# A table of selected rows in 112 rows, a searched order of work, and products of the identity in TensorE's gaps: block-sorted attention and a Fourier-mixing MLP

## The chip, the core and the metric

The kernel runs on one core of one Trainium2 chip. The engines have short names here: PE is TensorE's matmul side and PEld its weight loads, DVE is VectorE, ACT is ScalarE, POOL is GpSimd, SP is SyncE, which issues DMAs only. The metric is the device time of one execution in microseconds, as the median over runs: lower is better. The profile is of one execution, and its times count from the first instruction. PEclk in a profile is the share of TensorE's clock that was granted.

## What is computed

The reference has two halves. The first is attention in blocks: of 4 batches and 8 heads, each with 768 tokens of 64 features, the tokens are cut into 8 blocks of 96. A small 8 by 8 matrix per head is normalised five times by rows and columns and mixes the blocks of k and v; then each block of q attends to its mixed block. The second half takes the 512 features of all heads, adds the real part of a two-dimensional Fourier transform (over tokens and features), normalises each token, and runs an MLP of width 2048.

```python
for _ in range(5):
    P = np.exp(P - P.max(-1)); P = P / P.sum(-1); P = P / P.sum(-2)
k_sorted = einsum('bhij,bhjcd->bhicd', P, k_b)      # v likewise
attn = softmax(scale * q_b @ k_sorted.T)            # per block of 96
x = (attn @ v_sorted) as (4, 768, 512)
u = x + real(fft(fft(x, axis=1), axis=2))
un = (u - mean(u)) / sqrt(var(u) + 1e-6)
out = u + maximum(un @ w_ch1, 0) @ w_ch2
```

(The lines are shortened; the reference keeps the dimensions and adds 1e-9 to the sums.)

## The kernel before, in words

The kernel does not issue its work in the order of its source. Each piece (a few instructions on one engine) is given to a planner with `step` or `chain`: a name, the batch, the engines that could do it with a duration in nanoseconds for each, what it reads and what it writes. When all steps are known, `run` (L344) plays the program with its own clock: it keeps a time at which each engine is free, one for each DMA queue, and the buffers of each ring, and takes again and again the step that can start first, or of several within 40 ns (`NEAR`) the one of least priority number. `emit` (L279) then issues the step's instructions for good, so the order on each engine's queue is this order. The engines wait for each other through semaphores; the planner's times only decide the order and, where a step may run on several engines, the engine.

The priority of a step is its batch times 1e5 less the length of the work that hangs on it, plus 1000 times an entry of the table `LEAD` (L203), which holds for each name of a step four numbers, one for each batch. The entries are the result of a search.

The stages of a batch: k, q and v are loaded (`load_kq` on POOL's queue, `load_v` on SP's, L502), v is cast to half precision (`v_cast`, on ACT or DVE) and summed on POOL, the mixing matrix is spread out (`kron`), products with it give the mixed v and k (`psV`, `psK`, copies `vo`, `kz`), scores are computed twice (`psS` for the maxima, `psT` with the maximum taken off), ACT takes the exponentials (`exp`, tile `sm`), one is subtracted (`minus`, tile `eT`), POOL or DVE copies eight columns (`twice`, L850), and products with v give the attention (`psN`, L856). The Fourier transform over tokens folds the rows (`fold`, `fold2`) and multiplies with constant tables (L903), the one over features follows (L947 to L957). Then a row selection brings x into the order of the transform (`residual`, L984 and L987, with the constant table `rsel`), POOL adds (L1007, L1008), DVE takes mean and variance, `un` normalises (DVE, ACT or POOL, L1050 and L1053), the result is turned on PE (L1076) or by a DMA, and the MLP runs in two groups of 384 tokens (L1104 and L1125, with `relu` on ACT in between). MLP steps have the weakest priority: they fill what TensorE has free.

The table `rsel` is a constant in DRAM of 107 rows (96 + 11), each with 4 selections of 97 columns in half precision. It shares the tile `room` with small tables of the start, and is loaded by `load_const` (L1172) on SP's queue, not before 27 us of the planner's clock. Its price in the plan is `6 * elements // 1000 + 50` ns of transfer. Its rows 96 to 106 pick the mean rows; the products read 105 to 107 rows.

PSUM is eight banks of 512 columns. The ring `bank` hands them out singly and `pair` in twos; `open()` lists the free ones by the time at which they came free.

Early in the kernel, `warm` issues products of a tile of ones into bank 7, in three places before the planner's run starts.

Of the kernel before, what the change touches and what calls it, by code (L numbers as in the profile page):

```python
# [10 lines left out]
F16 = mybir.dt.float16  # L11
# [9 lines left out]
BLK = 96  # L21
G = 6
# [23 lines left out]
def _consts():  # L46

    p = np.arange(128)
    mask16 = (p[:, None] % 16 == np.arange(16)[None, :]).astype(np.float32)

    dd = np.arange(DM // 2)
    ang = 2.0 * np.pi * ((np.outer(dd, np.arange(2 * LT)) % DM) / DM)
    cd = np.stack([np.cos(ang), np.sin(ang)], 1)
    cd = np.concatenate([-cd[:, :, 1::2], cd[:, :, ::2], cd[:, :, 1::2]], -1)
    cd_hi = (cd / WSC).astype(np.float16)
    chunk = lambda m: np.ascontiguousarray(
        m.reshape(2, 128, 2, 3 * LT).transpose(1, 0, 2, 3))
    cd_hi = chunk(cd_hi)

    def trig(ss, kk):
        ang = 2.0 * np.pi * ((ss[..., None] * kk.reshape(-1)) % S) / S
        return np.stack([np.cos(ang), -np.sin(ang)], -2)
    krow = BLK * np.arange(4)[:, None] + KP[None]

    kpl = krow[[1, 2, 3, 0]]
    ss = BLK * np.arange(4)[None, :] + PERM[:, None]
    n_ = np.stack([PERM, BLK + (BLK - PERM) % BLK], 1)
    r_ = np.arange(8)  # L70
    j_ = np.minimum(r_, 7 - r_)

    def folded(kk, odd):
        t = np.concatenate([trig(n_, kk), np.zeros((8, 2, 2, kk.size))])
        t[0] = 0.0
        for e in range(2):
            sign = np.where((r_ > 3) & (e == 1), -1, 1) * np.where((j_ > 1) & (odd != e), -1, 1)
            t[BLK + r_, np.minimum(j_, 3 - j_), e] = sign[:, None] * trig(BLK * r_, kk)[:, e]
        m = trig(np.arange(S), kk).reshape(NB, BLK, 2, kk.size).sum(1)
        m[np.abs(m) < 1e-9] = 0.0  # L80
        hi = m.astype(np.float16).astype(np.float64)
        m = np.stack([np.concatenate([hi, m - hi, hi]), np.zeros((24, 2, kk.size))], 1)
        return np.concatenate([t, m]) * WSC
    cso = folded(kpl[:, 48:], 1).reshape(128, 2, 384).astype(np.float16)
    cse = np.concatenate(
        [folded(kk, 0) for kk in (np.array([384]), kpl[:, :24], kpl[:, 24:48])], -1)
    cse[:, :, 1, 0] = 0.0
    cse = cse.reshape(128, 2, 386).astype(np.float16)

    vrow = np.zeros((1, NB, 4, D + 1), np.float16)  # L90
    vrow[..., D] = BLK / XSC
    ones = np.ones((1, NB * (BLK + 16)), np.float16)

    low = np.zeros((128, 1), np.float32)
    low[16:24] = -1.0
    tok = np.zeros((8, BLK), np.int64)
    for (i, m), t in TILE.items():
        tok[t] = krow[i]
        if m:
            tok[t] = (S - krow[i] if i else np.append(S - krow[0, 1:], 384))  # L100
    tok = tok.reshape(6, 128).T
    idx = np.concatenate([tok + S * b for b in range(B)], 1)
    idx = np.ascontiguousarray(idx).astype(np.uint32)

    rsel = np.zeros((BLK + 11, 4, BLK + 1), np.float16)
    at = np.argsort(PERM)
    for v in range(2):
        for r, kr in enumerate(KP):  # L110
            p = at[(BLK - kr) % BLK if v else kr]
            rsel[p, 2 * v, r] = 1.0
            rsel[p if kr else BLK + 10, 2 * v + 1, r] = 1.0
    rsel[BLK + 10, 1::2, BLK] = 1.0
    rsel[BLK + 8, ::2, :BLK] = 1.0
    rsel[BLK + 8, 1::2, :BLK] = (KP != 0)[None]
    rsel[BLK + 9, 1::2, :BLK] = (KP == 0)[None]
    rsel[BLK + 9, 1::2, BLK] = 1.0

    qperm = np.zeros((128, 4, 4, 16), np.float16)  # L120
    for i in range(4):
        for c in range(16):
            qperm[32 * i + c, 0::2, i, c] = 1.0
            qperm[32 * i + 16 + 15 - c, 1, i, c] = 1.0
            qperm[32 * i + 16 + (16 - c) % 16, 3, i, c] = 1.0
    qperm = qperm.reshape(128, 256)
    nident = -np.eye(BLK).astype(np.float16)

    ij = np.arange(64)
    mask8 = (ij[:, None] // NB == np.arange(NB)[None]).astype(np.float32)  # L130
    selj = (ij[:, None] % NB == np.arange(128)[None] // 16).astype(np.float32)
    return (mask8, selj, mask16, cd_hi, cse, cso, low, vrow, ones, idx, rsel,
            nident, qperm)
# [64 lines left out]
class Plan:  # L198
# [1 line left out]
    LAG, PE_TAIL, MARGIN, NEAR = 45.0, 215.0, 120.0, 40.0  # L200
    PORT, PORT_WAIT = ("fold", "fold_d", "minus", "nm", "un", "v_cast"), 450.0
    SPARE = 2500
    LEAD = dict(We=(13.1, 0, 0, 0), Wo=(41, 0, 0, 0), a16=(5.5, 0, 0, -24), a24=(-37.2, 0, 0, 0),  # L203
        amr2=(0, -34.2, 0, 0), const=(-17.5, 0, 0, 0), exp=(0, 0, 3, 0), fold=(0, 17.2, 0, 17.1),
        fold2=(0, 0, -15.3, 0), kz=(0, 60, 0, -1.7), load_k16=(0, 1, -17.5, -60), load_q16=(0, 0, 0, -10.1),
        load_v=(0, 1.8, 0, 0), max=(0, -19.9, 53.2, 0), minus=(-50.1, 8.6, 0, 0), nm=(0, 0, -3, 0),
        norm=(-1.5, 0, 0, 0), ot=(0, 52, 0, 0), psK=(-38, 0, 0, 0), psQ=(0, 9.7, 0, 0),
        psR=(-30.3, 6.5, 49.1, 0), psS=(0, 7.2, 0, 28.9), psT=(-3.9, 4, 0, 0), psV=(-7.2, 16.3, 0, 0),
        psY=(-52.4, 0, 0, 0), twice=(0, 14.6, 0, 33.1), u=(0, 0, 41.6, 0), un=(0, 0, -24.6, 0),
        unT=(-20.4, 0, 0, 0), v_cast=(0, 47.8, 0, -10.4))  # L210
    DMA_AHEAD = 800

    def __init__(self, engines):
        self.engines, self.rings = engines, {}
# [62 lines left out]
            s.prio += 1e3 * self.LEAD.get(s.name, (0, 0, 0, 0))[s.b]  # L277

    def emit(self, s, e, at):  # L279
        for u in s.use + s.extra:  # L280
            if u.t is None:
                self.rings[u.tag].give(u)
        if s.bulk and e == "G" and self.began:
            for x in self.before(s) if s.bulk > 1 else ():
                self.wait_for(x)
            self.under_way.append(s)
        s.fn(e)
        s.by = e
        ns = s.on[e]
        if e == "T":  # L290
            ns -= self.TURNS * (self.half and s.name in self.HALF)
            self.half = s.name in self.HALF
        done = at + ns
        if e == "G" and not s.hop:
            self.pool = (at, done)
        self.free[e] = done if e in "TGS" else done - 60.0
        if s.hop:
            other = "G" if e == "S" else "S"
            begin = max(done, self.dma[e])
            ahead = max(0.0, self.dma[other] - begin)  # L300
            shared = min(s.work, ahead)
            self.dma[e] = begin + s.work + shared
            self.dma[other] += shared
            done = self.dma[e] + s.hop + min(2400.0, ahead)
            self.lanes[e] = self.lanes[e][s.lanes:] + [done] * s.lanes
            s.land = done
            done += self.SPARE
        s.fin = done + (self.PE_TAIL if e == "T" else self.LAG)
        for u in s.use:
            u.left -= 1  # L310
            u.free_at = max(u.free_at, s.fin)
# [81 lines left out]
def kernel(  # L393
# [10 lines left out]
    nc = tc.nc  # L404
# [8 lines left out]
    const = ctx.enter_context(tc.tile_pool(name="const", bufs=1))  # L413
# [8 lines left out]
    step, Buf = plan.step, plan.buf  # L422
# [144 lines left out]
             w=[(kron[b], half)])  # L567

    room = const.tile([128, 2 * BLK + 2], F32, name="rsel_sb")
    rsel = room.bitcast(F16)[0:BLK + 11].rearrange("p (v r) -> p v r", v=4)  # L570
    pw = room[0:32, 128:192].rearrange("p (i j) -> p i j", j=NB)
    nc.sync.dma_start(pw, sort_net.rearrange("b h i j -> (b h) i j"))
    mask8 = const.tile([64, NB], F32, name="mask8_sb")
# [270 lines left out]
    def values(n):  # L844
        b, h = divmod(n, H)
        pN, rz = Buf("pair"), Buf("rz")

        def twice(e):
            row = eT[n].t[0:BLK].rearrange("p i q -> p (i q)")
            plan.engines[e].tensor_copy(row[:, BLK:NB * (BLK + 16):BLK + 17], eT[n].t[0:BLK, :, 0])  # L850
        step("twice", b, {"G": 350, "V": 120}, twice, r=[(eT[n], y) for y in range(2)], w=[(eT[n], 2)])

        def f(e):
            ps = pair(pN, D + 1, BLK + 8)
# [188 lines left out]
    def normal(b, i, m):  # L1043
        n = rows(i)
        un[b, i, m] = Buf("un")

        def f(e):
            o, x = un[b, i, m].t[0:n], us[b, i, m].t[0:n]
            if e == "A":
                nc.scalar.activation(o, x, AF.Identity, scale=rstd[b, i].t[0:n, m:m + 1],  # L1050
                                     bias=nms[b, i].t[0:n, m:m + 1])
            else:
                plan.engines[e].tensor_scalar(o, x, scalar1=mv[b, i].t[0:n, m, 0:1],  # L1053
                                        scalar2=rstd[b, i].t[0:n, m:m + 1],
                                        op0=ALU.subtract, op1=ALU.mult)
        step("un", b, {"V": 690, "A": 814, "G": 1620}, f,
             r=[us[b, i, m], (mv[b, i], m), rstd[b, i], nms[b, i]], w=[un[b, i, m]])

    def transpose_u(b, i, m):
# [180 lines left out]
    for half in range(2):  # L1240
# [12 lines left out]
                "kron": [13500, 14200], "load_v": [4500, 6e3, 7500, 9500]})  # L1253

    copy_sums()
    for hp in range(4):
        load_v(1, hp, 32e3 + 2e3 * hp)
# [107 lines left out]
```

## Time and profile before

| what | value |
|---|---|
| median of 3 runs | 320.69 us (319.79 to 324.07) |
| the profiled execution's own time | 320.41 us |
| its span, first to last instruction | 318.6 us |
| mean granted clock of TensorE | 0.958 |
| bytes moved by DMA | 45.37 MB |
| chain that ended last: share of PE, of DMA | 47%, 12% |
| MLP products (L1104 and L1125), busy | 90.3 and 90.2 us |

A profile is read in this order here: the page gives the busy time of each engine and, in 40 equal slices, when it was busy and what clock was granted; stretches give the same for chosen times; the waits say who waited for whom; the timeline lists the instructions of an engine with the idle time ahead of each and what ended it, in square brackets; the chain that ended last is followed back from the last instruction. "SPq" is SP's queue of DMA issues: an issue has a time there, its landing is seen only where something waits for it.

### The profile page before, as it was taken

What the parts mean: (1) busy time and instruction counts of PE and PEld (TensorE: products, weight loads), DVE (VectorE), ACT (ScalarE), POOL (GpSimd) and SP (SyncE); (2) the same over time, 40 slices, a digit from 0 to 9 for tenths busy, and PEclk for the clock granted to TensorE, in tenths of its full rate; (3) what the DMA queues carried; (4) which work ended last, traced back from release to release, by engine and by line L of the source; (5) the groups of instructions that cost most, each with busy time, mean ns of one, the idle gap of its engine ahead of it and who ended that gap; (6) DMA issues with size and microseconds to landing.
All of it is one profiled execution on the core that took longest, in us unless ns stands there. A gap on an engine that the chain in (4) does not pass through costs nothing.

```text
span 318.6 us, 7297 instructions
## 1 busy us (share of the span) xinstructions
PE 286.2 (90%) x2619; PEld 184.6 (58%) x2619; DVE 224.8 (71%) x488; ACT 202.6 (64%) x474; POOL 173.9 (55%) x248
## 2 busy tenths in 40 slices
PE   8878479788997889999999999978999999999990
PEld 5657476675784545555666667635655654645540
DVE  5789568799999786697789999999775756111010
ACT  6566476768876476898789859866822764714500
POOL 8623385586898899774533535867423665112020
PEclk9999956987999999999999999999999999999996
DMA  7943963899579988779998544557544337424021
GB/s 219 181 119 84 217 127 50 122 172 217 156 118 236 191 212 238 150 112 184 202 195 151 133 129 98 142 140 193 127 97 131 104 79 231 108 68 132 0 93 39
DMA packets 56042, 45.37 MB, mean 142 GB/s; under 512 B 24996, under 2 KB 48142, under 8 KB 56006
## 3 DMA queue, kind: packets, MB, share of 16 engines
q1 hardware_dynamic: 41206, 28.35, 34.5%
q0 software_dynamic: 14800, 16.57, 30.0%
q8 instruction: 20, 0.33, 0.4%
q14 instruction: 16, 0.13, 0.1%
HBM read 34.60 MB, written 12.58 MB: 148 GB/s over the span
## 4 chain that ended last, share of the span: by engine, by line
PE 47%; DMA 12%; DVE 9%; POOL 7%; ACT 6%; issue 4%; POOLq 0%; DVEq 0%; ACTq 0%; SPq 0%
PE bank L1104 19%; PE bank L1125 13%; DMA out_dram<-outt,idx_sb 6%; DMA w2sb<-in_moe_w_ch_dram 2%; DMA eT<-es 2%; PE bank L856 2%; PE bank L903 2%; DVE st L1025 2%; DMA unT<-un 1%; ACT hr L1110 1%; DVE kz L493 1%; ACT kz L489 1%; POOL k L514 1%; POOL u L1007 1%; POOL u L1008 1%
## 5 line engine op out<-in xcount | busy, mean ns | idle before, releaser
L1104 PE MATMUL bank<-unT,w1sb 128*128 128x384 f16 x512 | 90.3, 326 | 0.5 <-DVE W L491 0.5
L1125 PE MATMUL bank<-w2sb,hr 128*128 128x512 f16 x384 | 90.2, 379 | 0.0
L1110 ACT ACTIVATE hr<-bank 128x384 f16<-128x384 f32 x128 | 59.8, 492 | 26.2 <-PE bank L1104 25.5
L1104 PEld LDWEIGHTS <-w1sb 128*128 128x128 f16 x512 | 48.4, 98 | 30.6 <-issue 0.6
L1125 PEld LDWEIGHTS <-hr 128*128 128x128 f16 x384 | 36.1, 98 | 38.9
L1148 POOL DMA_INDIRECT out_dram<-outt,idx_sb x23 | 23.5, 1023 | 58.7 <-DVE outt L1133 37.2
L1133 DVE SCALAR_TENSOR_TENSOR outt<-ur,bank 128x512 f32<-128x512 f32 x24 | 16.4, 684 | 36.1 <-PE bank L1125 36.0
L810 ACT ACTIVATE sm<-bank,mns 96x96 f32<-96x96 f32 x128 | 32.0, 339 | 2.9 <-DVE mns L815 2.6
L1025 DVE BATCH_NORM_STATS2 st<-u 96x6 f32<-96x512 f32 (+1 forms) x32 | 21.9, 684 | 7.1 <-POOL u L1008 7.0
L863 DVE TENSOR_TENSOR xr<-bank,rz 104x512 f16<-104x512 f32 x32 | 22.1, 691 | 1.1
L487 ACT COPY u<-bank 96x512 f32<-96x512 f32 (+1 forms) x23 | 13.2, 583 | 13.4 <-PE bank L984 9.3
L856 PEld LDWEIGHTS <-eT 97*104 97x104 f16 x256 | 16.9, 137 | 8.3 <-DVE eT L850 2.7
L856 PE MATMUL bank<-vs,eT 97*104 97x65 f16 x256 | 17.8, 220 | 4.1 <-DVE eT L850 3.7
L1053 POOL TENSOR_SCALAR un<-u,mv,rstd 96x512 f16<-96x512 f32 (+1 forms) x7 | 14.5, 2077 | 10.5 <-ACT hr L1110 3.8
L489 ACT ACTIVATE kz<-bank 64x768 f16<-64x768 f32 x19 | 15.2, 803 | 6.8 <-DVE kz L493 3.9
L533 POOL TENSOR_TENSOR v<-v 128x384 f32<-128x384 f32 x11 | 11.5, 1044 | 13.1 <-ACT v L487 9.3
L1007 POOL TENSOR_TENSOR u<-u,P 96x257 f32<-96x257 f32 (+1 forms) x16 | 11.8, 737 | 10.3 <-DVE P L965 6.7
L792 ACT ACTIVATE sm<-bank 96x768 f32<-96x768 f32 x16 | 12.7, 802 | 6.4 <-PE bank L787 6.1
L692 DVE SCALAR_TENSOR_TENSOR vo<-a,bank 128x384 f16<-128x384 f16 x32 | 16.0, 545 | 0.2
L487 ACT CAST W<-bank 128x384 f16<-128x384 f32 (+1 forms) x30 | 9.8, 372 | 9.8 <-PE bank L903 8.9
L815 DVE TENSOR_REDUCE mns<-bank 96x8 f32<-96x768 f32 x16 | 15.1, 944 | 1.2 <-ACT sm L810 0.6
L493 DVE TENSOR_SCALAR kz<-bank 64x768 f16<-64x768 f32 x13 | 12.3, 950 | 5.1 <-ACT kz L489 3.6
(141 smaller groups left out, 553.1 us busy)
## 6 DMA issues: line engine op xcount, KB each, us to landing
u_dram<-u SPq DMA_DIRECT2D x32, 192.0 KB
ur<-u_dram SPq DMA_DIRECT2D x24, 256.0 KB
v<-in_v_dram SPq DMA_DIRECT2D x11, 384.0 KB
vs<-vo SPq DMA_DIRECT2D x48, 65.0 KB
k<-in_k_dram POOLq DMA_DIRECT2D x15, 192.0 KB, 4.2
q<-in_q_dram POOLq DMA_DIRECT2D x15, 192.0 KB, 4.5
w1sb<-in_moe_w_ch_dram POOLq DMA_DIRECT2D x4, 512.0 KB, 8.7
w2sb<-in_moe_w_ch_dram POOLq DMA_DIRECT2D x4, 512.0 KB, 7.3
```

What stands on the lines that cost most here:

```text
L487: nc.scalar.copy(dst, src)
L489: nc.scalar.activation(dst, src, AF.Copy, scale=scale)
L692: ("vo", b, {"V": 560}, lambda e: nc.vector.scalar_tensor_tensor(vo[h // 4][:, :, h % 4, 0:D], a16s[b % 2].rearrange("p (h d) -> p h d", d ...
L810: nc.scalar.activation(sm.t[:, i], pair(pS, BLK)[:, y, i % 4], AF.Exp, bias=mn.t[:, i:i + 1], scale=-1.0)
L856: nc.tensor.matmul(ps[:, i // 4, i % 4], eT[n].t[0:97, i, 0:BLK + 8], vs[2 * (b % 2) + h // 4][:, i, (D + 1) * (h % 4):(D + 1) * (h % 4 + 1)])
L863: nc.vector.tensor_tensor(xr2[b % 2][0:BLK + 8, :, D * h:D * (h + 1)].rearrange("p (t j) d -> p t j d", t=2), ps[:, :, :, 0:D], r[:, :, :, ...
L1025: nc.vector.bn_stats(st.t[0:n], us[b, i, m].t[0:n])
L1104: nc.tensor.matmul(ps, w1sb[:, mc, 128 * fc:128 * fc + 128], unT[b, gr].t[:, mc, :], start=(mc == 0), stop=(mc == 3))
L1110: nc.scalar.activation(dst, bank(pH, [128, 384]), AF.Relu)
L1125: nc.tensor.matmul(ps, hr[f4].t[:, fc % 4, 128 * t:128 * (t + 1)], w2sb[:, fc, :], start=(fc == 0), stop=(fc == 15))
L1133: step("outt", b, {"V": 687}, lambda e, t=t, pC=pC, o=o: nc.vector.scalar_tensor_tensor(o.t, ur[t].t, RSC, bank(pC, [128, DM]), op0=ALU.mu ...
L1148: step("store", b, {"G": 1020}, lambda e: nc.gpsimd.indirect_dma_start(out=out.rearrange("b s m -> (b s) m"), out_offset=bass.IndirectOffs ...
```

## The change

Four things change, all in the order of work or in constants:

- `rsel` has 112 rows in place of 107, in DRAM, in the tile's view and so in the load. The five new rows are zeros; the products read the same rows as before.
- The planner's duration of `twice` on POOL goes from 350 to 270 ns, that of `un` on POOL from 1620 to 2080 ns.
- The table `LEAD` is another one: entries for 28 names, of which most names had other numbers before.
- In `emit`, before a step on TensorE is issued, the planner looks at the time for which TensorE would be idle on its own clock: from the end of TensorE's last step, or from 50 ns after the oldest free bank came free, if that is later, to the start of this step. Over 250 ns it issues products of the identity with itself (128 by 128, half precision) into that bank, 0.8 of the idle time divided by 56 ns in number. It does so for steps that start before 110,000 ns on the planner's clock, and only in its run. The results of these products are read by nobody.

```diff
-    rsel = np.zeros((BLK + 11, 4, BLK + 1), np.float16)
+    rsel = np.zeros((BLK + 16, 4, BLK + 1), np.float16)
...
-    LEAD = dict(We=(13.1, 0, 0, 0), Wo=(41, 0, 0, 0), a16=(5.5, 0, 0, -24), a24=(-37.2, 0, 0, 0),
...
+    LEAD = dict(P=(42.1, 0, 0, 0), Q=(0, 32.3, 0, 0), We=(0, 0.1, 0, -4.3), Wo=(0, 0.1, 0, 0),
...
+    IDLE, KEEP, ONE, UNTIL = 250, 0.8, 56.0, 110000
...
     def emit(self, s, e, at):
+        if e == "T" and self.began and at < self.UNTIL:
+            open_ = self.rings["bank"].open()
+            if open_:
+                idle = at - max(self.free["T"], open_[0][0] + 50.0)
+                if idle > self.IDLE:
+                    self.keep_busy(self.rings["bank"].tiles[open_[0][1]], int(self.KEEP * idle / self.ONE))
...
-    rsel = room.bitcast(F16)[0:BLK + 11].rearrange("p (v r) -> p v r", v=4)
+    rsel = room.bitcast(F16)[0:BLK + 16].rearrange("p (v r) -> p v r", v=4)
...
-        step("twice", b, {"G": 350, "V": 120}, twice, r=[(eT[n], y) for y in range(2)], w=[(eT[n], 2)])
+        step("twice", b, {"G": 270, "V": 120}, twice, r=[(eT[n], y) for y in range(2)], w=[(eT[n], 2)])
...
-        step("un", b, {"V": 690, "A": 814, "G": 1620}, f,
+        step("un", b, {"V": 690, "A": 814, "G": 2080}, f,
...
+    def keep_busy(t, count):
+        for _ in range(count):
+            nc.tensor.matmul(t[:, 0:128], ident, ident)
+    plan.keep_busy = keep_busy
```

More of the change, by code (lines that the diff above doesn't have):

```diff
@@ L202 @@
     SPARE = 2500
-    LEAD = dict(We=(13.1, 0, 0, 0), Wo=(41, 0, 0, 0), a16=(5.5, 0, 0, -24), a24=(-37.2, 0, 0, 0),
[L204 to L210, printed above, removed]
+    LEAD = dict(P=(42.1, 0, 0, 0), Q=(0, 32.3, 0, 0), We=(0, 0.1, 0, -4.3), Wo=(0, 0.1, 0, 0),
+        a16=(0, 0, 0, 57.3), a24=(0, -25.2, 0, 0), add=(0, 0, 8.7, 0), amr2=(8.9, 0, 0, -13.1),
+        exp=(0, 0, 17.5, 0), fold=(-32.4, 0, 41.2, -24.5), fold2=(-31.2, 0, 0, -34.7), kz=(1.7, 52.5, 0, 0),
+        load_k16=(0, -3.8, -1.9, 0), load_q16=(0, -34.2, -1.6, -27.5), max=(54, 0, 0, 0),
+        minus=(0, -8, 50.8, 3), psF=(30.4, 3.5, 0, 4.8), psK=(0, 0, 0, 15.9), psR=(7.6, 0, -10, 0),
+        psS=(55.3, -5.2, 0, 0), psT=(5.1, -15.7, 0, 0), psWe=(0, 0, 0, 46.1), psY=(2.9, 0, 0, 0),
+        psaT=(0, 7.5, 0, 0), stats=(-48, 2.1, 47.9, 0), twice=(0, 2.1, 0, -33.7), v_sum=(0, 0, -13.8, 0),
+        vo=(0, -38.1, 0, -28.7))
     DMA_AHEAD = 800
+    IDLE, KEEP, ONE, UNTIL = 250, 0.8, 56.0, 110000
     def __init__(self, engines):
```

## The prediction

> **What bounds the kernel now.** I read the page from the top (span, busy time, clock), then stretches of the span, then the waits and the order of work where the stretches look bad.
>
> ```profile
> span 318.6 us, 7297 instructions
> PE 286.2 (90%) x2619; PEld 184.6 (58%) x2619; DVE 224.8 (71%) x488; ACT 202.6 (64%) x474; POOL 173.9 (55%) x248
> PEclk9999956987999999999999999999999999999996
> ```
>
> PE is the busiest engine by far, and the clock row shows where it is not well used: the dips lie between slices 6 and 9, some 40 to 78 us. The busy time by stretch says the same in numbers (columns: PE, weight loads, DVE, ACT, POOL, then granted clock, DMA share, GB/s):
>
> ```profile
> 0.00:27.00 27.00, 21.27 (x248) 15.37 (x249) 20.69 (x60) 15.57 (x25) 15.42 (x27) 1.00 0.74 159
> 27.00:39.20 12.20, 7.71 (x155) 7.32 (x154) 9.27 (x16) 7.70 (x10) 3.42 (x10) 1.00 0.76 170
> 39.20:53.10 13.90, 11.95 (x108) 9.66 (x108) 8.91 (x21) 9.25 (x15) 9.56 (x14) 0.51 0.64 114
> 53.10:63.00 9.90, 7.86 (x138) 6.40 (x136) 8.10 (x17) 8.56 (x16) 6.67 (x11) 1.00 0.64 87
> 63.00:67.10 4.10, 4.10 (x49) 3.82 (x49) 3.86 (x8) 1.17 (x2) 3.64 (x6) 0.58 1.04 180
> 67.10:73.50 6.40, 4.67 (x74) 4.05 (x72) 5.69 (x15) 6.13 (x12) 3.64 (x6) 1.00 0.90 140
> 73.50:78.40 4.90, 4.68 (x27) 2.68 (x27) 4.45 (x11) 3.53 (x8) 4.03 (x4) 0.65 1.05 248
> 78.40:110.00 31.60, 28.91 (x307) 20.34 (x306) 28.50 (x63) 22.67 (x48) 26.93 (x37) 1.00 0.82 180
> 110.00:240.00 130.00, 124.58 (x1121) 76.71 (x1119) 109.30 (x228) 96.31 (x273) 75.73 (x109) 1.00 0.73 157
> 240.00:310.60 70.60, 70.51 (x411) 38.26 (x409) 25.32 (x55) 31.66 (x69) 24.24 (x28) 1.00 0.36 103
> ```
>
> From 110 us to PE's end at 310.6 PE idles 200.6 - 195.1 = 5.5 us; from 0 to 110 us it idles 110 - 91.15 = 18.85 us and runs 23 us at 0.51 to 0.65 of its clock. So the bound has two parts: TensorE from the point where the MLP can fill every gap (about 78 us), and before that a chain of waits through all engines. An earlier start of the second part moves the end by as much, as long as all engines move with it.
>
> The largest single hole of the first part is this (first the issues on SP, then ACT, then PE):
>
> ```profile
> 29.25 0.39 SPq L1172 DMA_DIRECT2D rsel_sb<-rsel  x1
> 29.69 0.70 SPq L506 DMA_DIRECT2D v<-in_v_dram  x1
> 36.64 0.55 SPq L700 DMA_DIRECT2D vs<-vo  x1
> ```
> ```profile
> SPq L700 <- DMA rsel_sb<-rsel: 1.4, 1, 1.4
> ```
> ```profile
> 32.71 0.84 ACT L839 ACTIVATE eT<-sm 96x768 f16<-96x768 f32 x1
> 37.63 0.83 ACT L487 CAST v<-v 128x768 f16<-128x768 f32 x1 [4.07 <-DMA v<-in_v_dram]
> ```
> ```profile
> 39.22 0.59 PE L784 MATMUL bank<-nident_sb,mxs 96*96 96x96 f16 x8 [3.90 <-ACT sm L792]
> 39.61 0.84 PE L787 MATMUL bank<-qT,kz 128*96 128x96 f16 x8
> 42.13 0.62 PE L856 MATMUL bank<-vs,eT 97*104 97x65 f16 x5 [1.69 <-DVE eT L850]
> ```
>
> The table rsel, in 107 rows, is issued by 29.64. SP's next wait for it ends at 36.64: 7.0 us. The v load issued right behind it lands at 37.63. The cast of v stands at the head of ACT's queue, the exponentials behind it wait 4.07 us, and PE waits 3.90 us for one of them. After its return PE has 0.51 of its clock until 53.1 (the third row above).
>
> Sizes and landings of transfers, for comparison:
>
> ```profile
> rsel_sb<-rsel SPq DMA_DIRECT2D x1, 81.1 KB
> k<-in_k_dram POOLq DMA_DIRECT2D x15, 192.0 KB, 4.2
> ```
>
> The 128-row k load moves 2.4 times the bytes and lands in 4.2 us. So 107 rows are slow for their bytes, 12 KB a microsecond, and v, behind it on the queue, is late with it.
>
> **The change, part by part.**
>
> *The table in 112 rows.* One DMA as before, 84.9 KB, five zero rows, no added instruction; products still read rows 0 to 106, so they cost the same. The planner's price for the load moves from 299 to 310 ns, nothing. What may go is the delay. Bounds: nothing, if the transfer stays as slow, and 4.07 us, if v is there when ACT asks at 33.55. Taken from the k row, rsel would land near 33.5 and v, with 384 KB but not blocked, near 34. I take 3.6 of PE's 3.90 us, leaving the few tenths that PE's other waits show. Late next is DVE's eT (1.69 us), which ACT's exponentials pace.
>
> [...]
>
> *The clock behind that hole.* The chain that ends last runs through PE in that stretch:
>
> ```profile
> 42.13 2.26 PE bank L856 x24
> 44.40 1.29 PE bank L903 x8
> 45.68 0.78 PE bank L722 x6
> 46.46 0.66 PE bank L740 x7
> ...
> 48.15 0.80 PE bank L768 x8
> ...
> 48.99 0.80 PE bank L768 x8
> 49.79 0.43 PE bank L984
> ...
> 51.92 0.44 PE bank L991
> ```
>
> With six products from 49.79 to 51.92 this is 2.26 + 1.29 + 0.78 + 0.66 + 1.60 + 2.59 = 9.18 us on the chain; at full clock half of it, 4.6 us, goes. But POOL is busy 9.56 us of the 13.90 and ACT 9.25, so the stretch cannot fall below 9.6: at most 4.3. At least nothing, if the 1.69 us wait halves the clock again. I take 3.4, nearer the upper end, because PE's work is the chain there and the products of the identity lie in the gap that is left.
>
> *The two shorter dips* (63.0 to 67.1 at 0.58, 73.5 to 78.4 at 0.65) follow short waits:
>
> ```profile
> PE bank L768 <- DVE kz L493: 1.3, 1, 1.3
> PE bank L947 <- ACT kz L489: 1.2, 1, 1.2
> ```
>
> At full clock PE would save 4.1 x 0.42 + 4.68 x 0.35 = 3.4 us, but DVE is busy 3.86 of 4.10 and 4.45 of 4.90 there, so 0.24 + 0.45 = 0.7 us is the most; at least 0. I take 0.5.
>
> [...]
>
> *The products of the identity.* Wherever the planner's own clock, up to 110 us, shows PE idle for over 250 ns, it now issues products of 128 columns into a free bank for 0.8 of the idle time, at 56 ns each. That price is the trace's at full clock:
>
> ```profile
> 181.00 0.45 PE bank L642 x8
> ```
>
> They are issued ahead of the step's real products on PE's in-order queue, after the last reader of that bank. In a gap as long as planned they cost nothing. The gaps they can fill: 18.85 us of idle before 110, less the hole (3.6) and the 5.73 of the first 27 us, most of it before the planner's run, are 9.5 us, so up to 7.6 us of products, some 135. If the gap is shorter than 0.8 of the plan, the overhang is added to PE, and at half clock the products take twice as long. Bounds: 0 and 7.6 us. I take 0.6, near the low end: PE's waits end on ACT and DVE work of steady length.
>
> *Durations and times.* These rows carry the correction that matters:
>
> ```profile
> L1053 POOL TENSOR_SCALAR un<-u,mv,rstd 96x512 f16<-96x512 f32 x5 | 10.4, 2075 | 10.2 <-ACT hr L1110 3.8 <-DVE Q L965 3.3 <-DMA unT<-un 1.7
> L1050 ACT ACTIVATE un<-u,nm,rstd 96x512 f16<-96x512 f32 x10 | 8.1, 813 | 2.4 <-DMA unT<-un 1.7 <-DVE nm L1039 0.5
> ```
>
> At 2080 in place of 1620 ns the planner gives POOL fewer of its un steps; each one moved takes about 0.8 us of ACT. The twice copy on POOL goes from 350 to 270 ns in the plan, which leaves it where it is. The new LEAD table shifts priorities by up to 55 us of the planner's clock, and may reorder any queue, SP's and POOL's loads included. The trace before cannot price that: its upper gain is the idle time left, its loss another hole like the one above. I take 0 and leave it to the rivals.
>
> **Sum.** Against the profiled execution's own 320.41 us (span 318.6 and 1.8 around it, 0.3 under the median of 320.69): 320.4 - 3.6 - 3.4 - 0.5 + 0.6 = 313.5 us. All of it is earned before 78 us; PE's 5.5 idle microseconds after 110 show that it is kept to the end only if the other engines start earlier too, which a shorter chain through all of them gives.
>
> **The rivals.**
> 1. *A denser order.* The search also takes half of the idle time that PE has from 78.4 to 240 us (2.69 + 5.42 = 8.1): 313.5 - 4 = 309.5. For it: the planner now knows what POOL's un takes. Against: DVE is busy 28.5 of 31.6 us there.
> 2. *The hole goes, the clock falls anyway*, because waits like the 1.69 us one remain: 320.4 - 3.6 + 0.6 = 317.4. For it: two dips here follow waits of 1.3 us.
> 3. *The change doesn't do what it says*: 112 rows land as late as 107, since DMA is 76% busy from 27 to 39 us anyway. The planner does not see that hole, so puts no products in it: about 320.5. Against: the k row.
> 4. *Slower: the products get in the way.* If the clock is not held, the 7.6 us of products take 15.2; if the gaps are half as long as planned (4.75), 10.4 us are displaced: 320.4 - 3.6 + 10.4 = 327.2. It ends above the kernel before from 3.6 us displaced, half the products. Against it: they stop at 110, and DVE's and ACT's durations are steady.
>
> **How the numbers follow.** The forecast (310.5 to 316.5) has 0.42, rival 1 0.20, rival 2 0.16, rival 3 0.08, rival 4 0.14. Two per cent, about what a measurement of this kernel can tell from no change, puts the bounds at 314.3 and 327.1. Two thirds of the forecast (0.28) and all of rival 1 are faster: 0.48. Rival 4 is over 327.1 a little more than half the time: 0.08. The rest, 0.44, is within 2%. The range 307 to 321 leaves out the lower end of rival 1 (0.05) and nearly all of rival 4 (0.13).
>
> **What would show it.** Right: SP's wait for rsel gone, no 4 us wait of ACT for v near 34 us, no PE gap over 2 us there, the clock row without its 5, the first L1104 before 73 us, and PE's end near 304. If the hole is gone but the clock row still falls, rival 2 holds. Products running on while the operands of the step behind them are long there show rival 4. The prediction is wrong if the new order holds a hole of its own, above all at a load that heads ACT's or POOL's queue, or if PE starves after 200 us because batch 3 is not ready earlier.

## The result, and the profile after

The changed kernel is slower. Over 20 runs each its median is 324.92 us (321.28 to 328.19), that of the kernel before 321.60 us (318.01 to 325.37); the ratio is 1.0098, with a 95% interval of 1.0070 to 1.0127. Forecast were 313.5 us and a range of 307 to 321, and both were missed. Ratios here and below compare only executions within 1.5% of the fastest of their kernel; in e7 these are 5 of 14, and its profile is of another one, so that experiment decides nothing.

The profiled execution took 323.39 us. Its page:

```profile
span 321.6 us, 7688 instructions
PE 292.2 (91%) x2814; PEld 189.7 (59%) x2814; DVE 223.1 (69%) x487; ACT 202.9 (63%) x477; POOL 178.0 (55%) x246
PEclk9999979999999999999999999999999999999997
```

PE has 195 more products and one shallow dip of its clock in place of four low slices. The same stretches as before, with the same columns:

```profile
27.00:39.20 12.20, 10.70 (x204) 9.93 (x202) 9.76 (x19) 9.62 (x13) 5.79 (x12) 1.00 0.77 155
39.20:53.10 13.90, 11.69 (x166) 9.82 (x166) 11.41 (x27) 9.69 (x18) 8.95 (x13) 0.88 0.76 149
63.00:67.10 4.10, 3.57 (x67) 3.45 (x64) 4.03 (x8) 3.17 (x6) 4.08 (x6) 1.00 0.93 177
73.50:78.40 4.90, 4.90 (x40) 3.35 (x39) 4.81 (x13) 3.41 (x9) 4.90 (x7) 1.00 0.60 175
78.40:110.00 31.60, 27.96 (x344) 20.97 (x342) 27.20 (x56) 20.71 (x41) 22.50 (x32) 1.00 0.83 169
110.00:240.00 130.00, 123.44 (x1116) 74.95 (x1114) 104.44 (x222) 96.64 (x279) 76.98 (x108) 1.00 0.72 152
```

The clock is held where it fell: 0.88 in place of 0.51, and 1.00 in both short stretches. But PE idles 3.64 us from 78.4 to 110 (2.69 before) and 6.56 from 110 to 240 (5.42 before), and 74 of the products stand in the first of these two stretches. The hole near 36 us, on SP, ACT and PE:

```profile
30.50 0.59 SPq L513 DMA_DIRECT2D v<-in_v_dram  x1
...
37.30 0.49 SPq L1179 DMA_DIRECT2D rsel_sb<-rsel  x1
```
```profile
35.46 0.81 ACT L494 CAST v<-v 128x768 f16<-128x768 f32 x1
```
```profile
41.98 1.35 PE L863 MATMUL bank<-vs,eT 97*104 97x65 f16 x24 [2.08 <-DMA vs<-vo]
```

The cast of v no longer waits. The new order also issues the table after the v load that this cast reads, so the table could not have been in its way here. PE's longest wait in this place is now 2.08 us, for the moves of mixed values (vs<-vo) that heads 4 to 6 need. Its longest in the whole execution comes late, for POOL's copy of eight columns (`twice`):

```profile
219.79 0.58 PE L863 MATMUL bank<-vs,eT 97*104 97x65 f16 x8 [2.79 <-POOL eT L857]
```

From about 270 us on PE runs nothing but MLP products, without a gap, so the MLP work done by then decides the end:

```profile
272.02 10.40 PE bank L1111 x64
282.42 10.36 PE bank L1132 x48
```

A product of L1111 is thus 162.5 ns, one of L1132 215.8 ns (L1104 and L1125 in the kernel before). Counts of both by time, first of the changed kernel, then of the kernel before (L1111 or L1104, then L1132 or L1125; the number after x is the count):

```profile
0.00:130.00 130.00, 18.07 (x99) 0.99 0.78 165
0.00:150.00 150.00, 23.55 (x128) 0.99 0.80 165
0.00:270.00 270.00, 68.95 (x384) 0.99 0.72 153
```
```profile
0.00:130.00 130.00, 11.53 (x48) 0.99 0.78 165
0.00:150.00 150.00, 21.71 (x89) 0.99 0.80 165
0.00:270.00 270.00, 67.58 (x280) 0.99 0.72 153
```
```profile
0.00:130.00 130.00, 20.92 (x114) 0.92 0.78 166
0.00:150.00 150.00, 23.63 (x128) 0.93 0.80 164
0.00:270.00 270.00, 70.36 (x392) 0.96 0.72 154
```
```profile
0.00:130.00 130.00, 11.69 (x48) 0.92 0.78 166
0.00:150.00 150.00, 21.62 (x90) 0.93 0.80 164
0.00:270.00 270.00, 69.12 (x288) 0.96 0.72 154
```

By 130 us that is 99 x 0.1625 + 48 x 0.2158 = 26.4 us of MLP work, against 28.9 before; by 270 us it is 122.8 against 125.8. These 3.0 us are the difference of the two spans. The MLP itself begins 3 us earlier than before (75.3 us, not 78.4), and by 105 us this lead is gone. The 2.5 us missing at 130 are not yet the loss: other work was done in their place, for at 150 us the two kernels are nearly level (40.0 and 40.2). Against the kernel before, the 3 us are lost between 150 and 270.

### The profile page after: what moved, and what is told of

Read it like the earlier page. It is cut to its first block, busy times and chain, and to the rows that moved or that the text cites. A ratio compares the mean times of both kernels' runs of the same rounds, so it can differ in the third digit from the quotient of the medians.

```text
span 321.6 us, 7688 instructions
## 1 busy us (share of the span) xinstructions
PE 292.2 (91%) x2814; PEld 189.7 (59%) x2814; DVE 223.1 (69%) x487; ACT 202.9 (63%) x477; POOL 178.0 (55%) x246
## 4 chain that ended last, share of the span: by engine, by line
PE 49%; DVE 15%; DMA 14%; ACT 7%; POOL 6%; issue 4%; SPq 2%; POOLq 0%; DVEq 0%; ACTq 0%
PE bank L1111 20%; PE bank L1132 17%; DMA eT<-es 5%; DMA out_dram<-outt,idx_sb 3%; PE bank L863 2%; DVE mxs L778 2%; DMA hr<-in_v_dram 2%; DMA vs<-vo 2%; PE bank L1264 2%; POOL u L1014 2%; POOL u L1015 1%; DMA u_dram<-u 1%; ACT kz L496 1%; DVE x L894 1%; DVE xs L889 1%
## 5 line engine op out<-in xcount | busy, mean ns | idle before, releaser
L1111 PE MATMUL bank<-unT,w1sb 128*128 128x384 f16 x512 | 90.1, 326 | 0.7 <-DVE xr L870 0.4
L1132 PE MATMUL bank<-w2sb,hr 128*128 128x512 f16 x384 | 90.6, 379 | 0.0
L1117 ACT ACTIVATE hr<-bank 128x384 f16<-128x384 f32 x128 | 60.7, 491 | 28.4 <-PE bank L1111 27.7
L1111 PEld LDWEIGHTS <-w1sb 128*128 128x128 f16 x512 | 48.3, 98 | 31.1 <-issue 1.3
L1132 PEld LDWEIGHTS <-hr 128*128 128x128 f16 x384 | 36.0, 98 | 37.7 <-issue 0.3
L889 POOL TENSOR_TENSOR xs<-xr 104x512 f16<-104x512 f16 x13 | 16.0, 1230 | 18.7 <-DVE xr L870 13.7
L863 PE MATMUL bank<-vs,eT 97*104 97x65 f16 x256 | 16.7, 215 | 9.0 <-POOL eT L857 3.1
L863 PEld LDWEIGHTS <-eT 97*104 97x104 f16 x256 | 15.0, 130 | 14.4 <-POOL eT L857 4.8
L1060 POOL TENSOR_SCALAR un<-u,mv,rstd 96x512 f16<-96x512 f32 (+1 forms) x8 | 17.1, 2132 | 9.2 <-PE bank L1083 4.1
L496 ACT ACTIVATE kz<-bank 64x768 f16<-64x768 f32 x20 | 16.1, 807 | 6.4 <-DVE kz L500 5.9
L494 ACT CAST W<-bank 128x384 f16<-128x384 f32 (+1 forms) x34 | 11.7, 385 | 12.1 <-PE bank L910 9.9
L894 DVE TENSOR_TENSOR x<-xs 104x512 f16<-104x512 f16 x32 | 15.2, 514 | 4.0 <-POOL xs L889 3.5
L846 ACT ACTIVATE eT<-sm 96x768 f16<-96x768 f32 x14 | 11.7, 842 | 5.4 <-PE bank L863 4.8
```

What stands on the lines that cost most here:

```text
L494: nc.scalar.copy(dst, src)
L496: nc.scalar.activation(dst, src, AF.Copy, scale=scale)
L863: nc.tensor.matmul(ps[:, i // 4, i % 4], eT[n].t[0:97, i, 0:BLK + 8], vs[2 * (b % 2) + h // 4][:, i, (D + 1) * (h % 4):(D + 1) * (h % 4 + 1)])
L889: step("fold", b, {"V": 425, "G": 1450}, lambda e, y=y, op=op: plan.engines[e].tensor_tensor(f1.t[:, y], xr[0:BLK + 8, 0:4, ms], xr[0:BLK ...
L894: nc.vector.tensor_tensor(f2.t[0:BLK + 8, :, 2 * y:2 * y + 2].rearrange("p j f m -> p f j m"), f1.t[:, :, 0:2], f1.t[:, :, 3:1:-1], op=op)
L1111: nc.tensor.matmul(ps, w1sb[:, mc, 128 * fc:128 * fc + 128], unT[b, gr].t[:, mc, :], start=(mc == 0), stop=(mc == 3))
```

## The experiments

Each run keeps one or two parts of the change. "Order" is what LEAD and the two durations decide. Where an edit must not move the order, the planner's price of the table's load was held; the instructions of PE, DVE, ACT and POOL are then the same, one by one. In the expectations "the table with the products" is e3.

**e1: the table alone**, order of before.

```diff
+    rsel = np.zeros((BLK + 16, 4, BLK + 1), np.float16)
+    rsel = room.bitcast(F16)[0:BLK + 16].rearrange("p (v r) -> p v r", v=4)
```

> The kernel before with nothing changed but the table of selected rows in 112 rows (its price in the plan held at 299 ns, so that the order of work on every engine is that of before). Theory A (the late v load was the table's doing; the order and the products lost the gain): SP's 1.4 us wait for the table and ACT's 4.07 us wait for v go, PE's 3.90 us hole shrinks below 1 us, and the time falls by 3 to 7 us to 315 to 318. Rival B (112 rows land as late, or v is late anyway on busy DMA queues): the hole stays and the time is that of before, within 1 us.

Measured: ratio 0.9987 (0.9951 to 1.0024), 0.4 us with about 1.2 on either side. The timelines of SP, ACT and PE:

```profile
30.23 0.54 SPq L1172 DMA_DIRECT2D rsel_sb<-rsel  x1
30.81 0.42 SPq L506 DMA_DIRECT2D v<-in_v_dram  x1
```
```profile
34.55 0.83 ACT L487 CAST v<-v 128x768 f16<-128x768 f32 x1 [0.52 <-DMA v<-in_v_dram]
```
```profile
41.24 2.26 PE L856 MATMUL bank<-vs,eT 97*104 97x65 f16 x24 [4.22 <-DMA idx_sb<-idx]
```

Theory A holds for the load and fails for the time. ACT's wait for v falls from 4.07 to 0.52 us, and PE's hole is as long as ever, only later. The profile puts it down to the load of idx, which landed last, but these products read eT and vs: they wait for the moves of mixed values, as the next runs name it. Heads 4 to 6 start at 41.24 in place of 42.13, so 0.9 us is all that this place gives.

**e2 and e3: the products alone, and table with the products**, both in the order of before.

```diff
+                if idle > self.IDLE:
+                    self.keep_busy(self.rings["bank"].tiles[open_[0][1]], int(self.KEEP * idle / self.ONE))
```

> The kernel before with the products of the identity alone, in its own order, table in 107 rows. Theory A (products planned after about 78 us push MLP work back, 56 ns each): what they save in the clock ahead of 78 us is given back, time within 2 us of before or above it. Rival C (the products are free and hold the clock; the new order costs the time): 2 to 4 us under before.

> The kernel before with the table in 112 rows and the products, in the order of before. Theory A: not better than the table alone, up to 4 us worse. Rival C: better than the table alone by 2 to 4 us, near the 313.5 that was forecast.

Measured: 0.9963 (0.9925 to 1.0001) and 0.9855 (0.9797 to 0.9913), the second at a median of 317.39 us. The 1.2 us of e2 fit theory A (within 2 us) and miss rival C's 2 to 4; e3 decides for rival C, 4.2 us better than the table alone: the products do not cost time in this order. Together the two parts gain 1.45%, some 4.7 us, more than the 0.4 and 1.2 us that they gain alone, neither of them clear of noise. In e3 the gap ahead of heads 4 to 6 is 1.47 us with products in front of it:

```profile
39.69 1.32 PE L863 MATMUL bank<-vs,eT 97*104 97x65 f16 x24 [1.47 <-DMA vs<-vo]
```

SP had issued the moves of their values by 35.92 us there and by 37.26 in e1, which is 1.3 of the 1.5 us by which they start earlier. Why SP was earlier is not shown by one profile of each.

**e4: the changed kernel without products.**

```diff
-    IDLE, KEEP, ONE, UNTIL = 250, 0.8, 56.0, 110000
+    IDLE, KEEP, ONE, UNTIL = 250, 0.8, 56.0, 0
```

> The changed kernel without the products, its order and its table otherwise the same. Theory A: the 74 products from 97 to 109 us (4.1 us at 56 ns) go and the time falls by 1 to 4 us against the changed kernel, even if the clock dips more early on. Rival C: the clock falls in the gaps ahead of 75 us and the time rises by 2 to 4 us over the changed kernel.

Measured: 1.0072 (1.0029 to 1.0114), against 1.0098 with them: 0.8 us better, less than theory A's 1 to 4, with intervals that overlap, and not the loss that rival C expected. In the changed kernel four groups of products, 5.1 us in all, lie on the chain that ended last:

```profile
24.61 0.61 PE bank L1264 x8
...
46.13 1.68 PE bank L1264 x15
...
104.38 1.73 PE bank L1264 x31
...
108.09 1.06 PE bank L1264 x19
```

Yet leaving all of them out buys 0.8 us and not 5.1. The clock falls again in the same order, which may be the reason. Stretches of e4, where the changed kernel has 1.00 in both:

```profile
67.10:73.50 6.40, 4.08 (x30) 2.35 (x29) 6.33 (x18) 4.83 (x10) 2.36 (x2) 0.80 1.14 214
73.50:78.40 4.90, 4.90 (x37) 3.26 (x36) 4.32 (x11) 3.04 (x8) 4.71 (x7) 0.91 0.66 172
```

So the products are about neutral in the new order. What remains is the order: 0.9855 with the old one, 1.0098 with the new one, all else equal, is 2.4 points (hundredths of the time before) or 7.8 us.

**e5 and e6: the two halves of the order**, each with table and products: the new durations under the old LEAD, and the new LEAD with the old durations.

```diff
-        step("un", b, {"V": 690, "A": 814, "G": 1620}, f,
+        step("un", b, {"V": 690, "A": 814, "G": 2080}, f,
```

> The kernel before with the table, the products and the two corrected durations, under the LEAD table of before: all of the change but the new LEAD. The table with the products, in the order of before, had a ratio of 0.9855 to the kernel before, the whole change 1.0098. Theory D (the new LEAD's order is what costs): 0.98 to 0.99. Rival E (any edit to what the planner reckons with, durations or LEAD, throws the order that the old LEAD was searched for, and the new orders are draws that are mostly worse): 0.995 to 1.02.

> The changed kernel with the old durations of the two steps: table, products and new LEAD. Theory D: as slow as the changed kernel, 1.00 to 1.02 times before. Rival E: another draw, anywhere from 0.99 to 1.03, and not tied to the changed kernel's 1.0098. If the new durations were the cause it would fall to 0.98 to 0.99.

Measured: 1.0249 (1.0184 to 1.0314) and 1.0371 (1.0293 to 1.0449). Theory D, the LEAD as the one cause, falls: each half alone is worse than both. Rival E stands as to the kind of thing that happens, another order after any edit to what the planner reckons with, but both times lie above its ranges (1.02 and 1.03).

**e7 and e8: no products after 75,000 ns of the planner's clock**, in the new and in the old order.

```diff
+    IDLE, KEEP, ONE, UNTIL = 250, 0.8, 56.0, 75000
```

> The changed kernel with the products only up to 75,000 ns of the planner's clock, its order otherwise the same: the 74 products between 95 and 110 us go. Theory F (products beside MLP work push it back): 3 to 4 us under the changed kernel, ratio to before 0.998 to 1.001. Rival G (PE would have waited there anyway): within 1 us of the changed kernel, 1.006 to 1.012.

> The table and the products in the order of before, products only up to 75,000 ns of the planner's clock: 80 products between 90 and 110 us go. Theory F: 3 to 4 us better than with all products, ratio to before 0.973 to 0.978. Rival G: the same 0.9855, within 0.005.

Measured: e7 has a ratio of 0.9999 (0.9946 to 1.0052), where theory F had it, but a median of 325.49 us over all its runs, above the 324.92 of the changed kernel, so nothing follows from it. e8 has 0.9900 (0.9822 to 0.9977), no better than the 0.9855 with all products: in the old order theory F (0.973 to 0.978) gets no support, the late products displace nothing that shows.

**e9 and e10: the order switched at 130,000 ns of the planner's clock**, old then new, and new then old, with table and products.

```diff
+            if self.SWITCH and first > self.SWITCH:
...
+                        x.prio = x.prio2
...
+                            x.on["G"] = self.LATER[x.name]
```

> Table and products as in the change. Steps that start before 130,000 ns of the planner's clock are ordered by the old LEAD and durations (the same instructions in the same order as the table with the products, ratio 0.9855), those after by the new ones. Theory H (the new order loses its time ahead of 130 us: the trace of the changed kernel has 4.8 us less MLP work done by 130 us than that kernel, and 5.3 us less by 270): 0.98 to 0.995. Rival E (any other order is a draw, mostly worse, wherever it begins): 1.00 to 1.03.

> The other way round: the changed kernel's own instructions and order up to 130,000 ns of the planner's clock, the old LEAD and durations after. Theory H: the loss is there, 1.005 to 1.015, and MLP work done by 130 us is about 26.4 us as in the changed kernel against 31.2 in the table with the products. If it comes below 0.995, the loss sits after 130 us.

Measured: 1.0148 (1.0072 to 1.0224) and 1.0388 (1.0316 to 1.0460). Theory H, that the loss sits ahead of 130 us, falls for e9, and e10 is far above its 1.005 to 1.015 too. The counts of e9 by 130 and 270 us (the lines are L1129 and, second, L1150 in it):

```profile
0.00:130.00 130.00, 23.63 (x128) 0.99 0.82 174
0.00:270.00 270.00, 71.30 (x384) 0.99 0.71 154
```
```profile
0.00:130.00 130.00, 12.72 (x52) 0.99 0.82 174
0.00:270.00 270.00, 67.02 (x283) 0.99 0.71 154
```

It has done 32.0 us of MLP work by 130 us, as good as any kernel here, and 123.5 by 270, where e3 has 128.1 (406 and 288 products). It is still 0.9 us ahead of e3 at 180 us (61.4 and 60.5) and 6.3 us behind at 210 (76.1 and 82.4). The early lead is no promise; the second half of the order can lose it again.

**e11 and e12: two v loads behind the moves of mixed values on SP's queue**, with the table, without and with products.

```diff
+            (held.append if b == 1 and hp in HOLD else lambda x: x())(g)
...
+                if b == 0 and half == 1 and g == G - 1:
+                    while held:
+                        held.pop(0)()
```

> The kernel before with the table in 112 rows; two loads of v for batch 1 are issued on SP's queue behind the last six moves of mixed values (vs<-vo) in place of ahead of them. All other engines keep their instructions and order. In the run with the table alone PE's hole was as long as before (4.22 us, to 41.24) and ended when heads 4 to 6 had their mixed values. Theory J (these moves, late on SP's queue behind the v loads, are what held PE there): PE's wait for them falls below 2 us and the time falls by 1 to 4 us under the table alone, ratio 0.986 to 0.996. Rival K (then ACT waits for v as long, or the queues are simply full): the hole stays near 4 us, ratio 0.995 to 1.003.

> The same with the products of the identity. Theory J: better than the table with the products, 0.972 to 0.984. Rival K: 0.983 to 0.99.

Measured: 1.0049 (1.0000 to 1.0098) and 1.0081 (1.0026 to 1.0135). Rival K is right about the hole, which stays, but both times lie above its ranges (0.995 to 1.003, and 0.983 to 0.99). ACT and PE in e11:

```profile
39.62 0.83 ACT L487 CAST v<-v 128x768 f16<-128x768 f32 x1 [6.12 <-DMA v<-in_v_dram]
```
```profile
41.21 0.80 PE L792 MATMUL bank<-nident_sb,mxs 96*96 96x96 f16 x8 [5.95 <-ACT sm L800]
```

With the values first, v is late, and heads 4 to 6 (at 42.45 us) no longer wait. Either way PE resumes at 41.2. Values and v are both needed by then and share the queue, so which of them goes first chooses who waits. With products the choice is not neutral: e12 differs from e3 in these two loads alone, PE waits 4.36 us in its place, and it is 2.3 points slower.

**e13 to e16: what an order is worth.** e13 is e3 with one constant of the planner moved by a nanosecond; e14 and e15 have an empty LEAD with old and new durations; e16 is the new order alone, table in 107 rows and no products.

```diff
-    LAG, PE_TAIL, MARGIN, NEAR = 45.0, 215.0, 120.0, 40.0
+    LAG, PE_TAIL, MARGIN, NEAR = 46.0, 215.0, 120.0, 40.0
```

> Table and products under the old LEAD and durations, with the planner's margin LAG at 46 in place of 45 ns: nothing else. The order of work departs from the old one after the first dozens of instructions. Rival E (orders are draws): slower than the 0.9855 of the same kernel with LAG 45, between 1.00 and 1.04. Theory D (old LEAD and old durations make good orders as such): 0.98 to 0.995.

> Table and products, old durations, LEAD empty. Rival E: 1.01 to 1.05, the level of an order that was not searched. Theory D: LEAD matters little as such, 0.985 to 1.00.

> Table and products, new durations, LEAD empty. Rival E: 1.01 to 1.05, so that the new LEAD (1.0098) still gained over no search. If it comes out at 0.99 or below, the new durations are better and the new LEAD made them worse.

> The new LEAD and durations alone: table in 107 rows (planner's price held at 310 ns, so that the order is that of the changed kernel), no products. The order then costs what it costs without help from table and products. Theory: 1.005 to 1.015, as with the table (1.0072), since this order issues the table behind the v loads. If the table's 7 us sit in front of other loads there, 1.015 to 1.03.

Measured: e13 1.0339 (1.0285 to 1.0394), e14 1.0633 (1.0573 to 1.0693), e15 1.0761 (1.0679 to 1.0843), e16 1.0087 (1.0043 to 1.0131). One nanosecond in a constant that prices no part of the change costs 4.8 points against e3. e14 and e15 lie above the 1.05 that rival E allowed. Each order has holes of its own; the longest wait in the tables of waits of e13 and of e15 (who waited for whom: us in total, times, longest):

```profile
PE bank L863 <- DVE eT L857: 9.2, 4, 5.9
```
```profile
PE bank L856 <- DMA vs<-vo: 7.3, 2, 6.7
```

e16 shows that the new order costs the same without table and products as with the table alone (1.0072), where the table goes behind the v load anyway. So the new order by itself costs 0.9 points, 2.8 us, and the table and the products, which gain 1.45 points in the old order, gain nothing in it (1.0087 without them, 1.0098 with them).

## Why the prediction was wrong

**The order, taken as 0: this step failed.** The prediction said of the new LEAD and durations "I take 0 and leave it to the rivals", and the rivals held only a gain from it (309.5) and a loss from the products (327.2). Measured with table and products on both sides, the new order costs 2.4 points, 7.8 us, more than the other terms together gain. Of these, 0.9 points are the order alone (e16), and nearly all the rest is the gain of table and products, which does not appear in it. So the order was not only mis-sized: the other terms hung on it, where the sum added them as if they did not. The view of the order as a neutral reshuffle was wrong for a reason that the runs show: the old order was a searched one. Without LEAD the same kernel stands at 1.063, the old LEAD brings it to 0.9855, and a nanosecond beside it gives back 4.8 points. Under the new durations the level without LEAD is 1.076, and the new LEAD reaches 1.0098: 6.6 points better than none, and still short of the order that it replaces. The prediction had named the danger, "another hole like the one above", and gave it no rival and no price. By its own terms such a hole is 3.9 us of waiting and 3.4 us of slow clock, 7.3 us; that this is near 7.8 is luck, since the runs show no single hole of that size, and 313.5 + 7.3 = 320.8 would still lie 4 us below the measured time. It also called the 11 ns in the planner's price of the table nothing; e13 shows that one nanosecond can redraw the order, and what the 11 do was not measured alone.

**The table, -3.6 us.** The delay was named right for v: with 112 rows ACT's wait falls from 4.07 to 0.52 us. The term was mis-sized because "late next" was misnamed. The prediction named DVE's eT, 1.69 us; late next were the moves of mixed values, and PE's hole was 4.22 us again. Alone the table is worth 0.4 us in the old order; under the products, from 0.9963 (e2) to 0.9855 (e3), it is worth about 3.5 us, and in the new order nothing (e16 against e4). In e1 v, issued right behind the table, landed some 3.7 us after its issue and not 7.9. Why the load in 107 rows takes so long, no run shows: that 112 rows land like the 128 of the k load was an estimate, and the landing of the table itself, which nothing waits for in e1, is not seen there.

**The clock, -3.4 and -0.5 us.** That the products hold it was right where they are issued: 0.88 and 1.00 in place of 0.51, 0.58 and 0.65. In e3 none stands from 63 to 75 us, and the clock falls to 0.73 although none of PE's waits up to 80 us is longer than 1.5 us:

```profile
67.10:73.50 6.40, 5.22 (x35) 2.98 (x33) 5.86 (x13) 5.13 (x11) 4.23 (x5) 0.73 0.99 199
```

But a held clock is not yet a gain. The products alone (e2) hold it at 1.00 in all three stretches and bring 1.2 us, not 3.9. In e4 the clock falls to 0.80 behind waits of PE of 1.4 us and less (below, its longest from 55 to 75 us), and in the changed kernel, which has products in the gaps of this order, it stays at 1.00 from 53.1 to 110 us. The length of one wait does not decide it: in the kernel before a wait of 1.24 us that ends at 71.95 us stands ahead of the dip to 0.65, and one of 1.23 us that ends at 103.17 us leaves the clock at 1.00 (from there to 106 us). What does decide it, no run shows.

```profile
PE bank L954 <- ACT kz L496: 1.4, 1, 1.4
PE bank L1083 <- DVE P L972: 1.2, 1, 1.2
```

**The products, +0.6 us.** No run shows this term by itself, since whatever time the products displace comes together with the clock that they hold. Clock and products together were forecast at -3.4 - 0.5 + 0.6 = -3.3 us. Measured are -4.2 us in the old order with the table (e3 against e1), -1.2 with the old table (e2) and +0.8 in the new order (against e4), the last two not clear of noise. Rival 4, the only slower rival, was not what happened. The 5.1 us of products on the chain that ended last look like its proof; e4 shows that this is not their price.

**The sum.** Table, clock and products without the order term were forecast at -6.9 us; e3 measures -4.7 (0.9855). That part had the right sign and two thirds of its size, 317 us and not 313.5, inside the range. This is in part luck: alone the two changes bring 0.4 and 1.2 us, and what they bring together is no sum of these. The signs that the prediction named divide the same way: SP's wait for the table is gone, ACT's for v too, and the clock row has no 5. But the first MLP product comes at 75.3 and not before 73, a gap over 2 us remains at 41.98, and PE ends near 313.5, not 304.

**What stays open.** Which step of the new order costs most was not isolated. As far as MLP work measures it, its lag behind e3 is 1.0 us at 95 us, 3.4 at 110, 4.8 at 130, 3.0 at 180 and 5.3 at 270, so it opens between 95 and 130 and, after a part is made good, again behind 180. PE's waits from 78 to 111 us, those over 0.2 us in total, are these, in the changed kernel and, second, in e3:

```profile
PE bank L910 <- DVE x L894: 1.1, 3, 0.7
PE bank L863 <- DVE eT L857: 0.9, 1, 0.9
PE bank L863 <- ACT sm L799: 0.7, 1, 0.7
PE bank L1083 <- DVE un L1060: 0.7, 1, 0.7
```
```profile
PE bank L910 <- DVE x L894: 0.6, 2, 0.3
```

These are many small waits and no single hole. Whether the new table was searched for just this kernel is not on record. e9 shows that a good start does not secure the end, so a place where the order goes wrong may not exist.

## What to carry to other kernels

An order of work that was searched is part of the kernel's speed, and everything that feeds the planner (a duration, a margin, a priority) redraws it: here one nanosecond cost 4.8 points, three times what the table and the products gain together. So make physical edits with the order held fixed, compare the instructions of each engine to be sure of it, and judge a new search only against the order that it replaces, on the chip. When a wait is removed, look for who reads the next thing on the same queue: here the hole that two transfers shared moved and did not close (PE came back at 41.24 us in e1 and at 41.21 in e11). The best version found here is the old order with the table in 112 rows and the products: 0.9855 of the time before (0.9797 to 0.9913).

## What the runs showed of the hardware

The transfer behind the table on SP's queue was late when the table had 107 rows: the cast of v started 7.9 us after the issue of its load in the kernel before and 7.6 us in e2, and with 5 rows of zeros added to the table ahead of it 3.7 us in e1 and 4.8 us in e3. The granted clock from 67.1 to 73.5 us was 0.80 in e4 and 0.73 in e3, behind waits of PE no longer than 1.4 us (e4, from 55 to 75 us) and 1.5 us (e3, up to 80 us); it was 1.00 in the changed kernel, which has the order of e4 and products in its gaps, and 1.00 in the kernel before from 103.17 to 106 us, behind a wait of 1.23 us. In the kernel before it was 0.50 from 42.0 to 53.1 us, although PE was busy for 10.7 of these 11.1 us.
